# Chunks 8 and 9 of a retention kernel by the DMA crossbar, with GpSimd holding the later loads

## The chip, the cores and the metric

One core of a Trainium2 chip. The metric is the device time of one launch in microseconds (us). Every comparison is with runs of the kernel before on the same chip, in the same rounds except for e6 to e8 (see The experiments); a ratio is the mean time of one kernel's fast runs over that of the other's fast runs of the same rounds, so it is not quite the ratio of the medians that are quoted beside it. The runs list one core, so there is no second one to compare its clock with, and "fast" here means not over 1.5% above the fastest run of the same kernel.

Words: SBUF is the core's memory for tiles, PSUM the memory, in banks, to which the products of this kernel go. "By the DMA crossbar" is said of a transfer that transposes (`dma_start_transpose` in the code). "To land" is to arrive, told from the issue of the transfer. TensorE "stands" while it waits between two products.

## The reference

A recurrent retention layer, then a gated feed-forward layer on its output. Shapes: q, k, v are 4 x 8 x 768 x 64 (batch, heads, tokens, head dimension), the feed-forward goes 512 to 1536 to 512 over 3,072 tokens.

```python
for t in range(S):                                     # retention, per head
    state = gamma * state + outer(k[t], v[t])
    y[t]  = scale * q[t] @ state
x    = y.transpose(0, 2, 1, 3).reshape(B * S, H * D)   # 3072 x 512
out  = (sigmoid(x @ w_gate) * (x @ w_val)) @ w_out
```

## The kernel before

The retention is done in 24 chunks of 128 tokens, six for each of the four sequences. The feed-forward takes four chunks (512 tokens, a "tile" t, six in all) at a time; while it works on tile t, blocks of two chunks each prepare the next tiles between its groups of products. The code takes both k and q into its products with the head dimension on the partitions, so each chunk's k and q are transposed: on TensorE, with a copy out of PSUM by ScalarE (chunks 4 to 9; chunks 0 to 3 have a path of their own), or by the DMA crossbar (chunks 10 to 23). In the profile of before one transpose on TensorE took 220 ns and a chunk's eight in a row 0.45 us, 56 ns each; the copy took 1.03 us of ScalarE per chunk.

```python
    def load_kq(g):                                    # GpSimd issues all loads, in order
        kn[g] = ld.tile([C, H, D], BF16, tag="kn", name="kn")        # 10 buffers
        qn[g] = ld.tile([C, H, D], BF16, tag="qn", name="qn")
        nc.gpsimd.dma_start(out=kn[g], in_=src(k, g))
        nc.gpsimd.dma_start(out=qn[g], in_=src(q, g))

    def transposes(g):                                 # by TensorE: 8 transposes, one copy
        tp = bank([128, 2 * NP, C], BF16)
        for i, x in enumerate((kn[g], qn[g])):
            for p in range(NP):
                nc.tensor.transpose(tp[:, i * NP + p, :], pair(x, p), ident)
        qkT[g] = at.tile([128, 2 * NP, C], BF16, tag="qkT", name="qkT", bufs=6)
        nc.scalar.activation(qkT[g], tp, AX.Copy)

    def xbar(g):                                       # by the crossbar, from the SyncE queue
        qkT[g] = ld.tile([128, 2 * NP, C], BF16, tag="qkX", name="qkX", bufs=8)
        for i, x in enumerate((kn[g], qn[g])):
            nc.sync.dma_start_transpose(out=qkT[g][:, i * NP:(i + 1) * NP, :],
                                        in_=x.rearrange("s h d -> s (h d)"))

    def casts(g):                                      # ScalarE: running state to bf16
        for i in range(g, g + 2):
            if i % NCH < NCH - 1:
                state_out(i, za[i])

    def block(done, new):                              # new: scores, state; done: y of the pair before
        for g in olds: inter(g)                        # y  = q @ cast state
        for g in news: scores(g)                       # needs qkT[g]
        for g in olds: intra(g)                        # y += masked scores @ v
        ...
        for i, g in enumerate(news):
            if g % NCH < NCH - 1:                      # the last chunk of a sequence has no state product
                state(g, zz[new][:, i], True)

    plan = {                                           # tile: (after which group, step)
        0: [..., (15, step_t, 8)],                     # step_t: transposes and v's scaling
        1: [(0, casts, 6), (1, step_t, 9), (3, block, 6, 8), (5, casts, 8), ...
```

In tile 1 the first six column groups are done in halves of 256 tokens, since only half of its input is there.

Of the kernel before, what the change touches and what calls it, by code (L numbers as in the profile page):

```python
# [9 lines left out]
F32 = mybir.dt.float32  # L10
BF16 = mybir.dt.bfloat16
# [6 lines left out]
def kernel(  # L18
# [10 lines left out]
    nc = tc.nc  # L29
    B, H, S, D = q.shape  # L30
    N_TOK, D_MODEL = out.shape
    D_FF = moe_w_gate.shape[1]
    C = 128
    NCH = S // C
    NP = H // 2
# [5 lines left out]
    ctx.enter_context(tc.manual_schedule())  # L41
    const = ctx.enter_context(tc.tile_pool(name="const", bufs=1))
    wpool = ctx.enter_context(tc.tile_pool(name="wpool", bufs=1))
    ld = ctx.enter_context(tc.tile_pool(name="ld", bufs=10))
    at = ctx.enter_context(tc.tile_pool(name="at", bufs=2))
    ffn = ctx.enter_context(tc.tile_pool(name="ffn", bufs=3))
    pz = ctx.enter_context(tc.tile_pool(name="pz", bufs=1, space=bass.MemoryType.PSUM))
# [2 lines left out]

    NG = B * NCH
    NT = N_TOK // 512
    XBAR = 10
    qn, kn, vf = {}, {}, {}

    def src(x, g):
        b, c = divmod(g, NCH)
        return x[b, :, c * C:(c + 1) * C, :].rearrange("h s d -> s h d")

    def load_v(g):  # L60
        vf[g] = ld.tile([C, H, D], F32, tag="vf", name="vf", bufs=8)
        nc.gpsimd.dma_start(out=vf[g], in_=src(v, g))  # L62

    def load_kq(g):
        kn[g] = ld.tile([C, H, D], BF16, tag="kn", name="kn")
# [4 lines that stand above are left out]
    def load_chunk(g):  # L70
        load_kq(g)
        load_v(g)
# [77 lines left out]
    xT, vs, qkT, sc, stA, stB, y, zbds = {}, {}, {}, {}, {}, {}, {}, {}  # L150
    zz, za = {}, {}

    def bank(shape, dt=F32):
        return pf.tile(shape, dt, tag="ff", name="ff")
# [12 lines left out]
    def xbar(g):  # L167
# [4 lines that stand above are left out]
# [68 lines left out]
    def x_cols(t, kk, lo, hi):  # L240
        if hi - lo == 512:
            return xT[t][:, :, kk, :]
        half = lo // 256
        return xT[t][:, half, kk, lo - half * 256:hi - half * 256]
# [29 lines left out]
    def new_run_T():  # L274
        return at.tile([128, NP, 2, C], BF16, tag="qkT", name="qkT", bufs=6)
# [104 lines left out]
    def up(t, n1, lo=0, hi=512, between=None):  # L380
        if t not in hT:
            hT[t] = ffn.tile([128, NFF, 512], BF16, tag="hT", name="hT", bufs=2)
        ps = []
        for w in (wg, wv):
            u = bank([128, 512])
            for kk in range(KT):
                nc.tensor.matmul(u[:, lo:hi], w[:, kk, n1 * 128:(n1 + 1) * 128], x_cols(t, kk, lo, hi),  # L387
                                 start=(kk == 0), stop=(kk == KT - 1))
            ps.append(u)
        if between:  # L390
            between()
        gs = ffn.tile([128, 512], F32, tag="gs", name="gs")
        nc.scalar.activation(gs[:, lo:hi], ps[0][:, lo:hi], AX.Sigmoid)  # L393
        nc.vector.tensor_tensor(hT[t][:, n1, lo:hi], gs[:, lo:hi], ps[1][:, lo:hi], op=ALU.mult)  # L394

    def up_columns(t, n1s, lo, hi, rows=1):
        if t not in hT:
            hT[t] = ffn.tile([128, NFF, 512], BF16, tag="hT", name="hT", bufs=2)
        n = hi - lo
        us = [bank([128, 512]), bank([128, 512])]  # L400
        for row in range(rows):
            for w, u in zip((wg, wv), us):
                for i, n1 in enumerate(n1s):
                    for kk in range(row * KT // rows, (row + 1) * KT // rows):
                        nc.tensor.matmul(u[:, i * n:(i + 1) * n], w[:, kk, n1 * 128:(n1 + 1) * 128],  # L405
                                         x_cols(t, kk, lo, hi), start=(kk == 0 and (rows == 1 or i == 0)),
                                         stop=(kk == KT - 1), skip_group_check=rows > 1)
        ps = [u[:, :len(n1s) * n] for u in us]
        gs = ffn.tile([128, 512], F32, tag="gs", name="gs")
        g = gs[:, :len(n1s) * n]  # L410
        nc.scalar.activation(g, ps[0], AX.Sigmoid)
        nc.vector.tensor_tensor(hT[t][:, n1s[0]:n1s[-1] + 1, lo:hi], g.rearrange("p (i n) -> p i n", n=n),
                                ps[1].rearrange("p (i n) -> p i n", n=n), op=ALU.mult)
# [18 lines left out]
    def keep_on(n, u):  # L432
        for _ in range(n):
            nc.tensor.matmul(u, ident, ident4, start=True, stop=True)  # L434

    def last_down(t):
        row = t * 512 + 384
        first = 0
        for i, width in enumerate((256, 128, 128)):
            o = bank([128, 512])  # L440
            for n1 in range(NFF):
                nc.tensor.matmul(o[:, :width], hT[t][:, n1, 384:512], wo[:, n1, first:first + width],  # L442
                                 start=(n1 == 0), stop=(n1 == NFF - 1))
            ob = ffn.tile([128, width], F32, tag=f"ob{width}", name="ob", bufs=2)
            if i == 1:
                nc.scalar.copy(ob, o[:, :width])
                nc.scalar.dma_start(out=out[row:row + 128, first:first + width], in_=ob)
            else:
                nc.vector.tensor_copy(ob, o[:, :width])
                nc.sync.dma_start(out=out[row:row + 128, first:first + width], in_=ob)  # L450
            first += width
# [14 lines left out]
    load_gate_val(2)  # L466
    scale_run(1, nc.gpsimd)
    warm = bank([128, 4, 128])
    keep_on(8, warm)
    kT[0], qT[0], kT[1], qT[1] = (new_run_T() for _ in range(4))  # L470
    transpose_run(kr[0], kT[0], [nc.scalar])
    state_run(0)
# [58 lines left out]
    def ups(t):  # L531
        return [lambda n1=n1: up(t, n1) for n1 in range(NFF)]

    def downs(t):
        return [lambda sm=sm, i=i: down(t, sm, i) for sm in range(4) for i in range(2)]

    plan = {
        0: [(9, step_t, 4), (10, step_t, 5), (11, block, None, 4), (12, step_t, 6), (13, casts, 4), (13, step_t, 7),
            (14, block, 4, 6), (15, step_t, 8)],
        1: [(0, casts, 6), (1, step_t, 9), (3, block, 6, 8), (5, casts, 8), (7, scale_v, 10), (9, scale_v, 11),  # L540
            (11, block, 8, 10), (13, casts, 10), (14, scale_v, 12), (15, scale_v, 13), (18, block, 10, 12),
            (20, casts, 12)],
        2: [(0, scale_v, 14), (1, scale_v, 15), (4, block, 12, 14), (6, casts, 14), (11, scale_v, 16),
            (12, scale_v, 17), (16, block, 14, 16), (18, casts, 16)],
        3: [(3, scale_v, 18), (4, scale_v, 19), (6, block, 16, 18), (8, casts, 18), (12, scale_v, 20),
            (13, scale_v, 21), (15, block, 18, 20), (17, casts, 20)],
        4: [(3, scale_v, 22), (4, scale_v, 23), (6, block, 20, 22), (8, casts, 22), (14, block, 22, None)],
        5: [],
    }
    for t in range(NT):  # L550
        groups = ups(t) + downs(t)
        if t == NT - 1:
            groups[-2:] = [lambda: last_down(t)]
        if t == 0:
            groups = groups[4:]
            for g in range(8, 12):
                load_chunk(g)
        if t == 1:
            groups[:6] = [lambda n1=n1: up(1, n1, 0, 256) for n1 in range(6)]
            groups[6:6] = [lambda n1=n1: up_columns(1, range(n1, n1 + 2), 256, 512) for n1 in range(0, 6, 2)]  # L560
            for g in range(12, 16):
                load_chunk(g)
        if t == 2:
            load_chunk(18)
            load_chunk(19)
        if t == 3:
            load_chunk(22)
            load_chunk(23)
        for i, group in enumerate(groups):
            if t == 1 and i == 0:  # L570
                for g in range(XBAR, 12):
                    xbar(g)
            if i == len(groups) - 9:
                for g in range(4 * t + 8, 4 * t + 12):
                    if 12 <= g < NG:
                        xbar(g)
            if t == 1 and i == len(groups) - 4:
                load_chunk(16)
                load_chunk(17)
            if t == 2 and i == len(groups) - 4:  # L580
                load_chunk(20)
                load_chunk(21)
            group()
            for at_group, step, *g in plan[t]:
                if at_group == i:
                    step(*g)
# [30 lines left out]
```

## Time and profile before

| | before |
|---|---|
| median of 4 runs | 231.56 us (231.24 to 231.97) |
| span of the profiled run | 229.2 us |
| TensorE busy | 220.8 us, 96% |
| first product of tile 1's first half group | 53.22 us |
| first half group after the block of chunks 6 to 9 | 59.94 us |

The lines of the page and of the chain are in the prediction below. A row of the chain reads: start, length, what the run waited for or did at that time. L387 and L405 are the up-projections, L423 the down-projection, L163 the transposes on TensorE, L184 the scores, L196 the product with the state (inter), L233 the product with v (intra), L202 the new state. In the changed kernel each of these lines has one number less.

One more view of the kernel before gives, for a stretch of time, the busy time of each engine and, as the last three numbers, TensorE's granted clock, the DMA share and the GB/s that the DMA engines moved. From 35 to 50 us, where the loads of chunks 6 to 11 run:

```profile
35.00:50.00 15.00, 15.00 (x123) 8.20 (x123) 6.87 (x12) 7.49 (x11) 13.48 (x16) 1.00 1.90 230
```

### The profile page before, as it was taken

The page shows a single profiled execution, that of the slowest core. Times are in us where ns is not written, and L with a number is a line of the kernel's source. Part 1 is how long each engine was busy: PE and PEld are TensorE (multiplying, and loading weights), DVE is VectorE, ACT ScalarE, POOL GpSimd, SP SyncE. Part 2 cuts the span into 40 slices and gives each one's busy share as a digit, 9 for nine tenths or more (in the row PEclk, how much of TensorE's full clock was granted, in tenths as well). Part 3 has the DMA queues.
Part 4 walks back from the last instruction along what each step waited for, and adds up shares of the span by engine and source line. Part 5 has one row for each costly group of instructions (what it writes and reads, how often), then busy time and mean ns, then how long its engine had stood idle before and what let it go on. Part 6 is the DMA issues. An engine that isn't in the chain of part 4 may idle for free.

```text
span 229.2 us, 4493 instructions
## 1 busy us (share of the span) xinstructions
PE 220.8 (96%) x1814; PEld 118.5 (52%) x1814; DVE 117.7 (51%) x223; ACT 89.0 (39%) x163; POOL 77.2 (34%) x99
## 2 busy tenths in 40 slices
PE   4889999999999999999999999999999999999994
PEld 1458544567775454454445445445445454444444
DVE  5587334358975927558426267637267520243301
ACT  5785332556362423426321532623432512434221
POOL 7899956998634462733410000000000000000000
PEclk9999999999999999999999999999999999999999
DMA  7999999999999999999999353012100012100022
GB/s 135 212 197 196 198 206 207 239 240 243 188 130 108 166 169 149 271 147 118 118 170 205 94 112 26 0 50 88 51 0 3 0 46 94 46 0 0 3 92 92
DMA packets 75476, 27.55 MB, mean 120 GB/s; under 512 B 62016, under 2 KB 71104, under 8 KB 75456
## 3 DMA queue, kind: packets, MB, share of 16 engines
q0 software_dynamic: 55440, 16.78, 68.6%
q1 hardware_dynamic: 19872, 10.43, 25.8%
q8 instruction: 14, 0.23, 0.4%
q10 hardware_dynamic: 144, 0.07, 0.1%
q14 instruction: 6, 0.05, 0.1%
HBM read 28.31 MB, written 6.29 MB: 151 GB/s over the span
## 4 chain that ended last, share of the span: by engine, by line
PE 89%; DMA 5%; ACT 2%; POOL 1%; DVE 1%; issue 1%; DVEq 0%; ACTq 0%
PE ff L387 50%; PE ff L423 26%; PE ff L405 4%; DMA wv<-in_moe_w_val_dram 3%; PE ff L233 2%; PE ff L184 2%; DMA vr<-in_v_dram 2%; PE ff L196 1%; PE ff L442 1%; PE ff L163 1%; PE z L202 1%; ACT zbd L208 1%; ACT qkT L165 1%; DVE vsr L279 1%; ACT gs L393 0%
## 5 line engine op out<-in xcount | busy, mean ns | idle before, releaser
L394 DVE TENSOR_TENSOR hT<-gs,ff 128x512 bf16<-128x512 f32 (+1 forms) x70 | 45.4, 656 | 61.2 <-PE ff L387 58.7
L387 PE MATMUL ff<-xT,wg 128*128 128x512 bf16 (+1 forms) x280 | 68.5, 367 | 0.0
L387 PE MATMUL ff<-xT,wv 128*128 128x512 bf16 (+1 forms) x280 | 68.5, 367 | 0.0
L393 ACT ACTIVATE gs<-ff 128x512 f32<-128x512 f32 (+1 forms) x70 | 40.0, 573 | 70.2 <-PE ff L387 64.2
L423 PE MATMUL ff<-wo,hT 128*128 128x512 bf16 x276 | 62.2, 380 | 0.0
L387 PEld LDWEIGHTS <-wv 128*128 128x128 bf16 x280 | 27.3, 98 | 29.9 <-DMA wv<-in_moe_w_val_dram 0.3
L423 PEld LDWEIGHTS <-hT 128*128 128x128 bf16 x276 | 26.4, 98 | 30.5
L387 PEld LDWEIGHTS <-wg 128*128 128x128 bf16 x280 | 26.8, 98 | 28.5
L428 ACT COPY ob<-ff 128x512 f32<-128x512 f32 x23 | 13.5, 585 | 49.0 <-PE ff L423 48.9
L62 POOL DMA_DIRECT2D vf<-in_v_dram x20 | 18.1, 903 | 24.6 <-DMA qn<-in_q_dram 7.9
L251 DVE TENSOR_TENSOR xT<-ff,taby 128x512 bf16<-128x512 f32 x20 | 12.9, 686 | 23.7 <-PE ff L233 23.7
L67 POOL DMA_DIRECT2D kn<-in_k_dram x20 | 17.9, 894 | 9.1 <-PE ff L387 4.6
L68 POOL DMA_DIRECT2D qn<-in_q_dram x20 | 17.8, 892 | 4.2 <-DMA wo<-in_moe_w_out_dram 1.6
L208 ACT CAST zbd<-za 64x256 bf16<-64x256 f32 x38 | 15.3, 403 | 7.7 <-DVE za L220 4.8
L175 DVE TENSOR_TENSOR vs<-vf,tabv 128x512 bf16<-128x512 f32 x20 | 13.4, 686 | 3.0 <-DMA vf<-in_v_dram 3.0
L189 DVE TENSOR_TENSOR stA<-ff,causal 128x512 bf16<-128x512 f32 x20 | 13.6, 682 | 0.0
L190 DVE TENSOR_TENSOR stB<-ff,causal 128x512 bf16<-128x512 f32 x20 | 13.6, 682 | 0.0
L434 PE MATMUL ff<-ident 128*128 128x512 bf16 x14 | 5.2, 504 | 3.0 <-POOL ident masks.py:199 3.0
L165 ACT ACTIVATE qkT<-ff 128x1024 bf16<-128x1024 bf16 x6 | 6.1, 1025 | 2.8 <-PE ff L163 2.7
L405 PE MATMUL ff<-xT,wg 128*128 128x256 bf16 x48 | 6.2, 273 | 0.7 <-DMA wg<-in_moe_w_gate_dram 0.7
L405 PE MATMUL ff<-xT,wv 128*128 128x256 bf16 x48 | 6.2, 273 | 0.2 <-DMA wv<-in_moe_w_val_dram 0.2
L233 PE MATMUL ff<-stB,vs 128*64 128x128 bf16 x80 | 6.3, 222 | 0.0
(85 smaller groups left out, 144.8 us busy)
## 6 DMA issues: line engine op xcount, KB each, us to landing
out_dram<-ob SPq DMA_DIRECT2D x23, 256.0 KB, 2.1
vf<-in_v_dram POOLq DMA_DIRECT2D x20, 256.0 KB, 10.7
kn<-in_k_dram POOLq DMA_DIRECT2D x20, 128.0 KB, 11.9
qn<-in_q_dram POOLq DMA_DIRECT2D x20, 128.0 KB, 11.6
wg<-in_moe_w_gate_dram POOLq DMA_DIRECT2D x6, 256.0 KB, 7.1
wv<-in_moe_w_val_dram POOLq DMA_DIRECT2D x6, 256.0 KB, 7.8
wo<-in_moe_w_out_dram POOLq DMA_DIRECT2D x4, 384.0 KB, 9.5
vr<-in_v_dram SPq DMA_DIRECT2D x1, 512.0 KB, 4.3
```

What stands on the lines that cost most here:

```text
L62: nc.gpsimd.dma_start(out=vf[g], in_=src(v, g))
L67: nc.gpsimd.dma_start(out=kn[g], in_=src(k, g))
L68: nc.gpsimd.dma_start(out=qn[g], in_=src(q, g))
L189: nc.vector.tensor_tensor(stA[g], sc[g][0], causal4, op=ALU.mult)
L190: nc.vector.tensor_tensor(stB[g], sc[g][1], causal4, op=ALU.mult)
L208: nc.scalar.copy(zbd[g % 4][half, :, half], z[half])
L387: nc.tensor.matmul(u[:, lo:hi], w[:, kk, n1 * 128:(n1 + 1) * 128], x_cols(t, kk, lo, hi), start=(kk == 0), stop=(kk == KT - 1))
L393: nc.scalar.activation(gs[:, lo:hi], ps[0][:, lo:hi], AX.Sigmoid)
L394: nc.vector.tensor_tensor(hT[t][:, n1, lo:hi], gs[:, lo:hi], ps[1][:, lo:hi], op=ALU.mult)
L405: nc.tensor.matmul(u[:, i * n:(i + 1) * n], w[:, kk, n1 * 128:(n1 + 1) * 128], x_cols(t, kk, lo, hi), start=(kk == 0 and (rows == 1 or i = ...
L423: nc.tensor.matmul(o, hT[t][:, n1, sm * 128:(sm + 1) * 128], wo[:, n1, :], start=(n1 == 0), stop=(n1 == NFF - 1))
L428: nc.scalar.copy(ob, o)
```

## The change

The intent: take the transposes of chunks 8 and 9 off TensorE as well, and keep the loads of later chunks from crowding the transposes. For the latter, GpSimd copies one element out of a transposed chunk before it issues the loads two chunks on; the copy is written to start once that transpose has landed, and in the profile of the changed kernel the seven copies stood 59.0 us in all for landings (`POOL gate L553 <- DMA qkX<-qn`). Fewer buffers do for k, q and v then.

```diff
-    ld = ctx.enter_context(tc.tile_pool(name="ld", bufs=10))
+    ld = ctx.enter_context(tc.tile_pool(name="ld", bufs=4))
-        vf[g] = ld.tile([C, H, D], F32, tag="vf", name="vf", bufs=8)
+        vf[g] = ld.tile([C, H, D], F32, tag="vf", name="vf", bufs=6)
-    keep_on(8, warm)
+    keep_on(9, warm)
 ...
-            (14, block, 4, 6), (15, step_t, 8)],
-        1: [(0, casts, 6), (1, step_t, 9), (3, block, 6, 8), (5, casts, 8), (7, scale_v, 10), ...
+            (14, block, 4, 6), (15, scale_v, 8)],
+        1: [(0, casts, 6), (2, scale_v, 9), (4, block, 6, 8), (6, casts, 8), (10, scale_v, 10), ...
 ...
+    gate = const.tile([1, 1], BF16, name="gate")
+
+    def load_behind(g):
+        nc.gpsimd.tensor_copy(gate, qkT[g - 2][0:1, 2 * NP - 1, 0:1])
+        load_chunk(g)
+        load_chunk(g + 1)
+
+    ahead = {(0, 14): [(xbar, 8), (xbar, 9), (load_behind, 10)],
+             (1, 0): [(xbar, 10), (xbar, 11), (load_behind, 12), (xbar, 12), (xbar, 13), (load_behind, 14)],
+             ...
-            groups[:6] = [lambda n1=n1: up(1, n1, 0, 256) for n1 in range(6)]
+            groups[:8] = [lambda n1=n1: up(1, n1, 0, 256) for n1 in range(8)]
```

More of the change, by code (lines that the diff above doesn't have):

```diff
@@ L52 @@
     NT = N_TOK // 512
-    XBAR = 10
     qn, kn, vf = {}, {}, {}
@@ L538 @@
         0: [(9, step_t, 4), (10, step_t, 5), (11, block, None, 4), (12, step_t, 6), (13, casts, 4), (13, step_t, 7),
-            (14, block, 4, 6), (15, step_t, 8)],
-        1: [(0, casts, 6), (1, step_t, 9), (3, block, 6, 8), (5, casts, 8), (7, scale_v, 10), (9, scale_v, 11),
-            (11, block, 8, 10), (13, casts, 10), (14, scale_v, 12), (15, scale_v, 13), (18, block, 10, 12),
-            (20, casts, 12)],
-        2: [(0, scale_v, 14), (1, scale_v, 15), (4, block, 12, 14), (6, casts, 14), (11, scale_v, 16),
+            (14, block, 4, 6), (15, scale_v, 8)],
+        1: [(0, casts, 6), (2, scale_v, 9), (4, block, 6, 8), (6, casts, 8), (10, scale_v, 10), (11, scale_v, 11),
+            (12, block, 8, 10), (14, casts, 10), (16, scale_v, 12), (17, scale_v, 13), (20, block, 10, 12),
+            (22, casts, 12)],
+        2: [(3, scale_v, 14), (4, scale_v, 15), (6, block, 12, 14), (8, casts, 14), (11, scale_v, 16),
             (12, scale_v, 17), (16, block, 14, 16), (18, casts, 16)],
@@ L549 @@
     }
+    gate = const.tile([1, 1], BF16, name="gate")
[5 more added lines that the diff above has]
+             (1, 0): [(xbar, 10), (xbar, 11), (load_behind, 12), (xbar, 12), (xbar, 13), (load_behind, 14)],
+             (2, 0): [(xbar, 14), (xbar, 15), (load_behind, 16)],
+             (2, 11): [(xbar, 16), (xbar, 17), (load_behind, 18)],
+             (3, 0): [(xbar, 18), (xbar, 19), (load_behind, 20)],
+             (3, 11): [(xbar, 20), (xbar, 21), (load_behind, 22)],
+             (4, 0): [(xbar, 22), (xbar, 23)]}
     for t in range(NT):
@@ L555 @@
             groups = groups[4:]
-            for g in range(8, 12):
-                load_chunk(g)
+            load_chunk(8)
+            load_chunk(9)
         if t == 1:
-            groups[:6] = [lambda n1=n1: up(1, n1, 0, 256) for n1 in range(6)]
-            groups[6:6] = [lambda n1=n1: up_columns(1, range(n1, n1 + 2), 256, 512) for n1 in range(0, 6, 2)]
-            for g in range(12, 16):
-                load_chunk(g)
-        if t == 2:
-            load_chunk(18)
-            load_chunk(19)
-        if t == 3:
-            load_chunk(22)
-            load_chunk(23)
-        for i, group in enumerate(groups):
-            if t == 1 and i == 0:
-                for g in range(XBAR, 12):
-                    xbar(g)
-            if i == len(groups) - 9:
-                for g in range(4 * t + 8, 4 * t + 12):
-                    if 12 <= g < NG:
-                        xbar(g)
-            if t == 1 and i == len(groups) - 4:
-                load_chunk(16)
-                load_chunk(17)
-            if t == 2 and i == len(groups) - 4:
-                load_chunk(20)
-                load_chunk(21)
+            groups[:8] = [lambda n1=n1: up(1, n1, 0, 256) for n1 in range(8)]
+            groups[8:8] = [lambda n1=n1: up_columns(1, range(n1, n1 + 2), 256, 512) for n1 in range(0, 8, 2)]
+        for i, group in enumerate(groups):
+            for step, g in ahead.get((t, i), ()):
+                step(g)
             group()
```

## The prediction

Passages of the record that rested on no trace or run of this case are cut from the text below, and from the expectation of e7, and each cut is marked. No term of the forecast's sum is among them: it stays -0.90 - 1.18 + 0.03 = -2.05 us. The 1.03 us per copy that its part 2 uses is the trace's, given above under The kernel before. Why transposes land later beside loads is not shown by any trace here; that they do is, with a median of 9.5 us over the whole run of before against 2.4 us from 120 to 140 us, where no load is issued.

> **What bounds the kernel now.** I read the busy shares first, then the chain that ended last, then the waits of TensorE, then the chain in order of time around the place that the change touches, and last the DMA landings of the transposes. The page of the kernel before (busy time per engine with its share of the span; then the chain's shares):
>
> ```profile
> PE 220.8 (96%) x1814; PEld 118.5 (52%) x1814; DVE 117.7 (51%) x223; ACT 89.0 (39%) x163; POOL 77.2 (34%) x99
> PE 89%; DMA 5%; ACT 2%; POOL 1%; DVE 1%; issue 1%; DVEq 0%; ACTq 0%
> ```
>
> TensorE is busy 220.8 of 229.2 us and carries 89% of the chain. The rest of the chain is mostly the start: loads of v and of a weight up to 15.9 us. After that there is little idle time to win; only work taken off TensorE, or the few places where it stands, can shorten the run. One such place is the chain in order of time (start us, us, what) between 52.9 and 60 us, where the transposes of chunks 8 and 9 lie:
>
> ```profile
> 52.94 0.45 PE ff L163 x8
> 53.38 1.75 PE ff L387 x16
> 55.13 0.45 PE ff L163 x8
> ...
> 56.07 0.40 ACT zbd L208
> 56.48 0.41 ACT zbd L208
> 56.89 0.01 issue
> 56.91 0.38 ACT gs L393
> 57.29 0.50 ACT qkT L165
> 57.79 0.30 issue
> 58.09 0.68 ACT gs L393 x2
> 58.77 0.04 issue
> 58.81 0.38 PE ff L184 x7
> 59.19 0.57 PE ff L233 x16
> ```
>
> The reader is to see two things. Each chunk transposed on TensorE costs 0.45 us of its time (eight matmuls). And from 56 to 58.8 us the chain runs over ScalarE, not TensorE: the casts, a sigmoid and the copy of chunk 9's transposes out of PSUM (L165) hold up the scores of chunks 8 and 9. The timeline of TensorE has the up-projection end at about 57.17 and the first product of the scores' successor (L233) at 59.12. Between lie 4 inter products (0.22 us by the chain's 0.22 for four) and 16 score products (0.55 us for 16). So 59.12 - 57.17 - 0.77 = 1.18 us is standing time.
>
> [...] The transposes' time from issue to landing (min/median/max us), first in the whole run, then from 120 to 140 us where no load is issued:
>
> ```profile
> DMA to landing us min/median/max: 2.4/9.5/13.1
> ```
> ```profile
> DMA to landing us min/median/max: 2.4/2.4/4.1
> ```
>
> Alone, 128 KB land in 2.4 us, against 2.1 us for a plain 256 KB store[...]; beside loads they take about four times as long[...]. That is what the gate is for: it keeps the next loads out of the way of the transposes.
>
> **The change part by part.**
> 1. Chunks 8 and 9 leave TensorE: 16 transposes, 2 x 0.45 = 0.90 us off the path, because TensorE is the path there.
> 2. Their two copies leave ScalarE (about 1.03 us each). The 1.18 us of standing before the scores had ScalarE as its cause; without 2.06 us of copies in 53.4 to 58.2 us, and with the block one group (0.88 us) later, I take it as gone: -1.18 us. The same wait for chunk 7's copy at 49.2 stays.
> 3. The second tile's first eight column groups, instead of six, are done in halves. Two groups of 512 columns cost 2 x 1.73 = 3.46 us (0.865 us for four matmuls, by the starts in the timeline); in halves 4 x 0.435 + 2 x 0.875 = 3.49 us: +0.03 us.
> 4. One more warming matmul at the start, about 0.4 us. TensorE then waits 0.44 us for the first k load anyway, and the chain there runs over v and a weight load until 15.9 us: 0.
> 5. Four more crossbar transposes, 1.3 us of the SyncE queue each, and seven tiny GpSimd copies as gates. SyncE and GpSimd are not on the path: 0 by themselves.
> 6. k and q get 4 buffers in place of 10, v 6 in place of 8. The order of instructions shows that the loads of chunk 8 now wait for TensorE to finish the state of chunk 4 (44.6 us by the chain: 44.37 + 0.25); before, k of chunk 8 was issued at 41.8 us. So the loads of 8 and 9 move back some 2.8 us.
> 7. The later blocks move one to two groups back. TensorE executes the same products in another order: 0 as long as nothing is late.
>
> Sum without a new wait: -0.90 - 1.18 + 0.03 = -2.05 us, so 229.6 us.
>
> **The rivals.**
> *A: the transposes of 8 and 9 come late and stall TensorE.* Loads are issued 0.88 us apart on GpSimd, so q of chunk 9, fifth of six, is issued at 44.6 + 4 x 0.88 = 48.1 us. Loads issued in 39 to 50 us landed after 6.2 to 7.7 us with a full queue behind them; with the pause of 2.8 us I estimate 5.5 to 6.5. It lands at 53.6 to 54.6. Its transpose is issued then and, the gate holding chunk 10 back until chunk 8 is through, should land 2.4 to 4 us later: 56 to 58.6 us. TensorE starts the second tile 0.45 us earlier than before (52.8), needs five half groups of 0.875 us, then 0.22 for inter and 0.27 for chunk 8's scores: it wants chunk 9 at 57.7. So the stall is 0 to 1 us, my mean 0.6. If the transposes are as slow as beside the old loads (7.4 to 12 us), it would be 3.5 to 5 us and eat the whole gain: 231 to 234 us.
> *B: the chain of gates is slower than TensorE later.* One turn of two chunks is six issues (5.3 us), about 5.5 us to landing and 2.5 us for the last transpose, with overlap about 11 to 13 us. The blocks want a pair at about 57, 71, 85, 102, 119, 136, 152 and 171 us (old chain shifted, with the new group numbers), never less than 13.5 us apart. So it keeps up; only the pair 10/11, wanted at 71 and ready by my estimate at 68 to 71, is close. Such a stall would not add to the first, since the gates do not wait for TensorE; the later of the two decides. Each would make 230 to 232 us.
> *C: the gain is hidden elsewhere.* For: 1.18 us of standing is short, and VectorE is fairly full from 50 to 65 us (3.7 to 4.7 of each 5 us by the table of stretches), so its masks might take ScalarE's place in holding TensorE. Against: the block now has three further half groups behind it before the whole-width work needs its y, where it had two. If only part 1 pays: 230.8 us.
> *D: gain over 2%.* It would need 4.6 us; TensorE's busy time forbids it.
>
> **Range and chances.** From 231.68: -2.05, +0.6 for A and some +0.1 for B and C, gives 230.3 us. Low end, all gains and no stall with noise of the runs (231.24 to 231.97 before): 229.2. High end, a stall of about 3 us at the first or second pair: 232.6. Slower by 2% (236.3) would need a stall of 6.5 us or a collapse of the transposes' pace: 0.03. Faster by 2% (227.1): 0.02. Within 2%: 0.95.
>
> **What the profile after would show.** L163's successor has 32 matmuls instead of 48 and the copy out of PSUM 4 instead of 6 of that shape. In the waits of TensorE, a wait of the score products for the DMA of qkX, of 0 to 1 us, near 57 us; over 2 us means rival A. The ScalarE pieces between 56 and 58.8 us are gone from the chain. GpSimd shows seven gate copies, waiting for qkX; the landings of the transposes have a median well under 9.5 us (4 or less if the gate works); the DMA row stays busy until about 165 us instead of 137. The prediction is wrong if the scores of chunks 8 to 11 wait long for the crossbar, or if TensorE stands just as long there for ScalarE or VectorE.

## The result, and the profile after

The changed kernel takes 230.89 us (median of 4 runs, 230.62 to 231.42) against 231.56 us: ratio 0.9973, interval 0.9949 to 0.9998. The time lies in the predicted range, but the predicted gain was 1.4 us and the measured one is 0.6 us. In a second set of five rounds (e1 below) it was smaller still.

The page of the changed kernel, busy times and shares of the chain:

```profile
PE 219.9 (96%) x1815; PEld 119.1 (52%) x1815; DVE 117.9 (51%) x224; ACT 87.0 (38%) x162; POOL 78.9 (34%) x106
PE 84%; DMA 10%; POOL 2%; issue 1%; DVE 1%; SPq 1%; DVEq 0%
```

TensorE works 0.9 us less, as the prediction had it. But TensorE's share of the chain fell from 89% to 84% and that of the DMA rose from 5% to 10%: transfers now hold TensorE. The chain in order of time shows where:

```profile
46.02 8.70 DMA kn<-in_k_dram
54.72 0.02 issue
54.73 1.19 SPq L169
55.92 0.04 issue
55.97 3.58 DMA qkX<-qn
59.54 0.14 issue
59.68 0.40 PE ff L183 x8
```

The load of chunk 9's k takes 8.7 us from its issue; then come the issues of its transposes on SyncE, then 3.58 us for the last one to land, and only then chunk 9's scores. The waits of TensorE (engine, line, for whom: us in total, times, longest) include three that the kernel before does not have:

```profile
PE ff L183 <- DMA qkX<-qn: 0.6, 1, 0.6
...
PE ff L162 <- DMA qn<-in_q_dram: 0.3, 1, 0.3
...
PE ff L386 <- DVE hT L393: 0.2, 1, 0.2
```

The second is for the load of chunk 7's q, a chunk that the change does not touch. The third is for PSUM banks: a half group of the up-projection can't start until VectorE has taken an earlier one out of its banks. The transposes themselves land as hoped; over the whole run, min/median/max us:

```profile
DMA to landing us min/median/max: 2.4/3.6/6.6
```

So the median is 3.6 us in place of 9.5. And here is the same stretch of 15 us as above:

```profile
35.00:50.00 15.00, 14.69 (x112) 7.74 (x111) 7.03 (x12) 7.24 (x11) 10.54 (x12) 1.00 1.81 207
```

207 GB/s in place of 230, in a stretch where the DMA engines are about as busy (1.81 and 1.90), and GpSimd comes to its first gate only at 48.7 us. This is the line that led to the cause.

### The profile page after: what moved, and what is told of

Read it like the earlier page. It is cut to its first block, busy times and chain, and to the rows that moved or that the text cites. A ratio compares the mean times of both kernels' runs of the same rounds, so it can differ in the third digit from the quotient of the medians.

```text
span 229.3 us, 4531 instructions
## 1 busy us (share of the span) xinstructions
PE 219.9 (96%) x1815; PEld 119.1 (52%) x1815; DVE 117.9 (51%) x224; ACT 87.0 (38%) x162; POOL 78.9 (34%) x106
## 4 chain that ended last, share of the span: by engine, by line
PE 84%; DMA 10%; POOL 2%; issue 1%; DVE 1%; SPq 1%; DVEq 0%
PE ff L386 47%; PE ff L422 23%; PE ff L404 5%; DMA kn<-in_k_dram 4%; DMA wv<-in_moe_w_val_dram 3%; PE ff L232 2%; PE ff L183 2%; DMA vr<-in_v_dram 2%; DMA qkX<-qn 2%; PE ff L195 1%; PE ff L441 1%; PE z L201 1%; DVE vsr L278 1%; SPq L169 1%; PE ff L162 0%
## 5 line engine op out<-in xcount | busy, mean ns | idle before, releaser
L393 DVE TENSOR_TENSOR hT<-gs,ff 128x512 bf16<-128x512 f32 (+1 forms) x70 | 44.8, 648 | 59.1 <-PE ff L386 53.4
L386 PE MATMUL ff<-xT,wg 128*128 128x512 bf16 (+1 forms) x280 | 67.6, 364 | 0.2 <-DVE hT L393 0.2
L386 PE MATMUL ff<-xT,wv 128*128 128x512 bf16 (+1 forms) x280 | 67.6, 364 | 0.1
L392 ACT ACTIVATE gs<-ff 128x512 f32<-128x512 f32 (+1 forms) x70 | 39.5, 567 | 67.7 <-PE ff L386 61.7
L427 ACT COPY ob<-ff 128x512 f32<-128x512 f32 x23 | 13.5, 585 | 49.2 <-PE ff L422 45.1
L553 POOL COPY gate<-qkX 1x1 bf16<-1x1 bf16 x7 | 1.6, 234 | 59.0 <-DMA qkX<-qn 59.0
L66 POOL DMA_DIRECT2D kn<-in_k_dram x20 | 17.9, 894 | 5.8 <-DMA qkX<-kn 1.5
L404 PE MATMUL ff<-xT,wg 128*128 128x256 bf16 x56 | 7.3, 273 | 1.1 <-DMA wg<-in_moe_w_gate_dram 1.1
L404 PE MATMUL ff<-xT,wv 128*128 128x256 bf16 x56 | 7.3, 273 | 0.1
L411 DVE TENSOR_TENSOR hT<-gs,ff 128x512 bf16<-128x512 f32 x7 | 4.7, 687 | 4.0 <-PE ff L404 3.9
```

The source lines that it names most:

```text
L386: nc.tensor.matmul(u[:, lo:hi], w[:, kk, n1 * 128:(n1 + 1) * 128], x_cols(t, kk, lo, hi), start=(kk == 0), stop=(kk == KT - 1))
L392: nc.scalar.activation(gs[:, lo:hi], ps[0][:, lo:hi], AX.Sigmoid)
L393: nc.vector.tensor_tensor(hT[t][:, n1, lo:hi], gs[:, lo:hi], ps[1][:, lo:hi], op=ALU.mult)
L404: nc.tensor.matmul(u[:, i * n:(i + 1) * n], w[:, kk, n1 * 128:(n1 + 1) * 128], x_cols(t, kk, lo, hi), start=(kk == 0 and (rows == 1 or i = ...
```

## The experiments

Sixteen runs were made, on three chips (e1 to e8 on one, e9 to e12 on another, e13 to e16 on a third). The runs of before are quoted with each; e5 to e8 are compared with the eleven of e1 to e4, made twelve minutes earlier on the same chip, and one more, so a drift is not excluded. The medians of before in the calls differ by up to 0.2 us (231.21 to 231.37; 231.56 in the first set), so times are compared within a call and ratios across calls. All results were correct.

### e1: the changed kernel again

> The changed kernel again, for a tighter interval and a second profile. Theory S (the standing of TensorE before the scores of chunks 8 and 9 was not removed but came back as a wait for PSUM banks of 0.6 us and a wait for the crossbar of 0.6 to 0.7 us): 0.5 to 0.8 us below the kernel before, ratio 0.9965 to 0.998. If instead the profiled run's start (0.25 us later) and its wait for q of chunk 7 (0.5 us) are part of the change and not noise, both show again; if they are noise, the wait for q of chunk 7 is absent or appears in the run of before too.

231.06 us against 231.29, ratio 0.9991 (0.9976 to 1.0006): a gain of 0.2 us that is not clear of the noise. With the first set, the change as it stands is worth something like 0.2 to 0.6 us. In this profile tile 0's down-projection began 0.3 us later than in the first, the delay by chunk 7's q was 0.25 us by the starts in the timeline (its transposes took 0.70 in place of 0.45 us; the table of waits doesn't list it), and the scores waited 1.20 us for the crossbar.

### e2: six buffers for k and q

```diff
-    ld = ctx.enter_context(tc.tile_pool(name="ld", bufs=4))
+    ld = ctx.enter_context(tc.tile_pool(name="ld", bufs=6))
```

> The changed kernel with 6 buffers for k and q in place of 4, so that the loads of chunks 8 and 9 do not wait for TensorE. Theory T1 (late crossbar is what ate the gain): the wait of the scores for the crossbar near 59 us goes, and the time falls by 0.5 to 0.8 us against the changed kernel (about 230.2). Rival T2 (the PSUM banks and ScalarE take the place of that wait): the wait for the crossbar goes, but TensorE then stands for VectorE or ScalarE, and the time falls by less than 0.3 us.

231.45 us against 231.29, ratio 1.0008 (0.9992 to 1.0025). The wait of the scores is still there, and longer:

```profile
PE ff L183 <- DMA qkX<-qn: 1.2, 1, 1.2
```

So the buffers are not what makes chunks 8 and 9 late. The timeline of GpSimd explains why: in the changed kernel the load of chunk 8's k was issued at 42.86 us and the fifth load (chunk 9's q) at 46.89, not at 44.6 and 48.1 as the prediction had them. The line there shows what ended GpSimd's short wait (last column):

```profile
42.86 0.87 POOL L66 DMA_DIRECT2D kn<-in_k_dram  x1 [0.20 <-PE ff L162]
```

It waited for transposes (L162), not for a state product: the first buffer to come free is that of chunk 5, the last of its sequence, which has no state product. With six buffers the issue was at 42.59 us. The loads start early enough; they land late.

### e3 and e4: the state casts two groups later, alone and with six buffers

```diff
-        1: [(0, casts, 6), (2, scale_v, 9), (4, block, 6, 8), ...
+        1: [(2, casts, 6), (2, scale_v, 9), (4, block, 6, 8), ...
```

> The changed kernel with the state casts of chunks 6 and 7 two groups later in ScalarE's order (after the third half group, not the first), so that ScalarE does not stand for VectorE at their head. T2: the waits of 0.6 us for PSUM banks at 57 us go. But if the crossbar comes at 59.5 us anyway (T1), the block waits just as long for it, and the time is within 0.3 us of the changed kernel.

> Both edits together. If the two waits hide each other (each alone gives little), this gives 1.0 to 1.4 us against the changed kernel, so about 229.6, which is the sum of the prediction. If T1 alone is right it is no better than the 6 buffers alone; if T2 alone is right, no better than the later casts alone.

e3: 230.75 us against 231.29, ratio 0.9995 (0.9962 to 1.0029); one of its runs, the profiled one, was at a clock of 0.993 and took 233.4 us, which widens the interval (in its trace the clock was at half from 61.4 to 64.8 us, right behind the waits for the crossbar). e4: 230.87 us, ratio 0.9997 (0.9968 to 1.0027), with one such run too. In both profiles the wait for PSUM banks near 57 us is gone and a wait for the crossbar remains (2.2 us over two places in e3, 0.63 us in e4). Neither reaches the 229.6 us hoped for; inconclusive as times, and as profiles they say that the crossbar's lateness is left.

### e5: the kernel before again, one look

> The kernel before once more, for a second profile of it. In five profiles of the changed kernel and its variants q of chunk 7 lands 1.7 us later than in the one profile of before (48.5 against 46.7 us), and already the weights land 0.3 to 0.8 us later. If this is noise of the runs, it shows here too or lies between; if it comes with the change, q of chunk 7 lands at about 46.7 us again and TensorE does not wait for it.

A single run of 230.65 us, whose state is unknown. Its profile served as the control: chunk 7's q landed at 46.5 us, as in the first profile of before (46.7), and TensorE did not wait for it. In each of the five profiles of the changed kernel and its variants so far it landed at 48.5 to 48.7 us. The slower loads therefore came with the change and not with the run.

### e6: only the casts of the kernel before moved

```diff
-        1: [(0, casts, 6), (1, step_t, 9), (3, block, 6, 8), ...
+        1: [(2, casts, 6), (1, step_t, 9), (3, block, 6, 8), ...
```

> The kernel before with only the state casts of chunks 6 and 7 moved two groups later in ScalarE's order. If the 1.18 us of standing before the scores was ScalarE being held at these casts by VectorE, part or most of it goes: 0.4 to 1.0 us faster. If it was the copies of the transposes, as the prediction had it, nothing changes (within 0.3 us).

231.17 us against 231.29, ratio 0.9996 (0.998 to 1.0012): nothing. The product with the state then waits for the casts itself:

```profile
PE ff L196 <- ACT zbd L208: 0.5, 1, 0.5
```

The two copies of transposes are still in ScalarE's queue, and moving the casts alone only moves the wait.

### e7: chunks 8 and 9 by the crossbar, without the rest

```diff
-    XBAR = 10
+    XBAR = 8
-            (14, block, 4, 6), (15, step_t, 8)],
-        1: [(0, casts, 6), (1, step_t, 9), ...
+            (14, block, 4, 6), (15, scale_v, 8)],
+        1: [(0, casts, 6), (1, scale_v, 9), ...
+            if t == 0 and i == 14:
+                xbar(8)
+                xbar(9)
```

> The kernel before with chunks 8 and 9 by the crossbar and nothing else of the change: old buffers, no gate, old places of the blocks. Theory: the transposes [...]land after 9 to 12 us instead of 4 to 6, and the scores wait for them at 57 us until 62 to 65 us: 4 to 7 us slower than before, and the gates are what makes the crossbar usable here. Rival: the gates do little at this place, the wait is 2 us or less and the time is within 1 us of before.

239.50 us against 231.29, ratio 1.0352 (1.0335 to 1.0369): 8 us slower. The waits of TensorE, and the clock row of the page:

```profile
PE ff L184 <- DMA qkX<-qn: 7.5, 2, 4.2
```
```profile
PEclk9999999999559999999999999999999999999999
```

The four transposes landed after 9.2 to 11.6 us (from 49 us on), beside loads of chunks 10 to 12 that nothing held; in the changed kernel those of chunks 8 and 9 landed after 3.6 to 6.4 us. TensorE stood 7.5 us, and two slices of the page ran at half the granted clock (0.68 on average from 55 to 70 us); the loss, 8.2 us by the medians, exceeds the wait. Loads issued beside them took longer still: those of chunks 11 and 12 landed after 13.5 to 17.9 us. So holding the loads, in one way or another, is what makes the crossbar usable at this place (e16 bears this out: there the buffers alone hold them). The granted clock fell at 60.3 us, 3.1 us into the first of two waits (3.3 and 4.2 us); in e3 and e10 it fell right behind waits of 2.2 us in all. What makes it fall, no run here shows.

### e8: later casts, and the block one half group later

```diff
-        1: [(0, casts, 6), (2, scale_v, 9), (4, block, 6, 8), (6, casts, 8), ...
+        1: [(2, casts, 6), (2, scale_v, 9), (5, block, 6, 8), (7, casts, 8), ...
```

> The changed kernel with the later casts, and the block of chunks 6 to 9 one half group later. If the wait for the crossbar (0.6 to 1.6 us in four profiles) is what is left of the lost gain, 0.87 us of it fills with a half group: 0.4 to 0.8 us faster than the later casts alone (230.7), about 230.1. If y of chunks 6 and 7 then comes too late for the whole-width columns, or loads simply set the pace, it is within 0.2 us of that.

230.42 us against 231.29, ratio 0.9966 (0.9946 to 0.9985). The scores no longer wait for the crossbar. This treats the symptom: the loads are as slow as in the changed kernel (all profiles at this placement of the tiles, e8's among them, moved 203 to 207 GB/s from 35 to 50 us; see the next part).

### e9, e10, e11: where the tiles lie

Why should loads of chunk 7, or of the weights, be slower in the changed kernel? Its one new tile is the gate: 2 bytes, which take 32 in SBUF, allocated ahead of the weights. In the built programs the first weight starts at byte 53,120 of each partition before and at 53,152 after, and every tile behind it is moved by the same 32 bytes.

```diff
 e9 (e11: 64 in place of 32)
-    gate = const.tile([1, 1], BF16, name="gate")
+    gate = const.tile([1, 32], BF16, name="gate")
-        nc.gpsimd.tensor_copy(gate, qkT[g - 2][0:1, 2 * NP - 1, 0:1])
+        nc.gpsimd.tensor_copy(gate[:, 0:1], qkT[g - 2][0:1, 2 * NP - 1, 0:1])
 e10, in the kernel before
+    pad = const.tile([1, 1], BF16, name="pad")
+    nc.vector.memset(pad, 0.0)
```

> The changed kernel with the gate's tile 64 bytes long in place of 2 (which takes 32). In the changed kernel the weights, k, q and v start 32 bytes further on in SBUF than before (53,152 in place of 53,120 for the first weight), no longer at a multiple of 64; with this edit they are at multiples of 64 again. Theory P (placement: the 32 bytes slow the loads): q of chunk 7 lands at 46.5 to 47.5 us, not 48.5, TensorE does not wait for it, the crossbar's last transpose for chunk 9 lands 1 us or more earlier, and the time falls by 0.6 to 1.2 us. Rival N (the slower loads come from elsewhere): landings as in the changed kernel, and the time within 0.3 us.

> The kernel before with an unused tile of 2 bytes (32 in SBUF) ahead of the weights, and nothing else. Theory P: the weights' last load lands 0.5 us later than before (about 28.4 us against 27.8), q of chunk 7 at about 48.4 us, TensorE waits for it 0.2 to 0.6 us, and the time rises by 0.3 to 1.0 us. Rival N: landings and time as before, within 0.3 us.

> The changed kernel with the gate's tile 128 bytes long, so that all loaded tiles start at multiples of 256 bytes. If what counts is that the start is a multiple of 64, as for e9 (within 0.2 us of it); if the transfers gain further from 256, landings another 0.3 us or more earlier.

The three came with the same runs of before, 231.37 us.

| kernel | loaded tiles start, past a multiple of 256 bytes | GB/s, 35 to 50 us | chunk 7's q lands, us | median us | ratio to before |
|---|---|---|---|---|---|
| before | 128 | 230 | 46.7 | 231.37 | 1 |
| e10 before, 32 bytes more | 160 | 204 | 48.5 | 232.65 | 1.0046 (1.0009 to 1.0083) |
| changed (e1) | 160 | 205 | 48.6 | 231.06 | 0.9991 |
| e9 changed, 64 byte gate | 192 | 205 | 48.4 | 231.34 | 0.9988 (0.9957 to 1.0018) |
| e11 changed, 128 byte gate | 0 | 230 | 47.4 | 230.22 | 0.9949 (0.9919 to 0.998) |

The rows for the stretch from 35 to 50 us, of the kernel before with 32 bytes of padding:

```profile
35.00:50.00 15.00, 14.75 (x111) 7.78 (x112) 7.01 (x12) 7.11 (x11) 11.54 (x14) 1.00 1.81 204
```

of the changed kernel with the 64 byte gate:

```profile
35.00:50.00 15.00, 14.63 (x111) 7.75 (x112) 6.99 (x12) 7.29 (x11) 10.54 (x12) 1.00 1.82 205
```

and with the 128 byte gate:

```profile
35.00:50.00 15.00, 14.89 (x118) 8.11 (x118) 7.05 (x12) 7.30 (x11) 10.74 (x13) 1.00 1.93 230
```

The last number of each row is the one to compare. Thirty-two bytes of padding slow the kernel before by about a tenth in this stretch of loads and cost it about 1 us (one of its runs, the profiled one, was slow and is not in the ratio; its granted clock was at half from 76.6 to 80.0 us, after the stretch that is read here). In that profile TensorE lost 0.32 us to chunk 7's q (by the starts) and stood 2.2 us for the late transposes of chunk 11, a wait that before does not have; the clock fell right behind it:

```profile
75.85 0.40 PE L184 MATMUL ff<-qkX 64*128 64x128 bf16 x8 [2.23 <-DMA qkX<-qn]
```

VectorE's and ScalarE's instructions took the same time on the moved tiles (gate times value, L394: 687 ns with and without the padding; the sigmoids of 128x512, L393: 597 ns in before and, moved by the same 32 bytes, in the changed kernel), so the tiles' own use is not what became slower.

My expectation that a multiple of 64 would do is refuted: e9 is as slow as the changed kernel. A multiple of 128 does. With it, chunk 9's last transpose landed at 57.0 us in place of 59.5, TensorE waited neither for it nor for chunk 7's q, and the gain of the change against before went from 0.2 to 0.6 us up to 1.15 us; against e9, e11 is 0.7 us faster by the means of the runs. In the stretch from 20 to 35 us, mostly weights, 200 or 201 GB/s moved in all of these, so the placement did not show there.

The kept traces hold every DMA packet with its size, queue and time (no view lists them), and they tell which loads it slows. From 35 to 50 us, the packets of 4,096 bytes, which are v's, took 172 to 181 ns on average in the nine profiles with tiles at 0 or 128, and 259 to 273 ns in the nine at 160 or 192. Those of 128 bytes, which are k's and q's, took 32 ns in all eighteen, and those of 512 bytes, the weights', 60 to 61 ns over the whole run. GpSimd's first load of v goes into a tile that the 32 bytes did not move, and its packets took 185 to 192 ns everywhere. So v's transfers are what the placement slows; k and q, whose loads are issued between v's, land later without being slower themselves.

A start 128 past a multiple of 256 did as well as a multiple of 256 here: the nine profiles at 0 or 128 moved 227 to 232 GB/s from 35 to 50 us, the nine at 160 or 192 moved 203 to 207. Why a target that starts at 160 or 192 takes v's packets longer, no run here shows.

### e12: the 64 byte gate with e8's two moves

```diff
 e9's edit and e8's edit together
```

> The changed kernel with the 64 byte gate, the later casts and the block one half group later together. If the loads then come early enough anyway, no better than the 64 byte gate with the block in its place plus what the casts' wait was (0 to 0.3 us); if each of the three waits found (for q of chunk 7, for PSUM banks, for the crossbar) was worth its time, about 229.5 to 230.0 us, 1.3 to 1.8 below before, which is near the sum of the prediction.

230.01 us against 231.37, ratio 0.9937 (0.9908 to 0.9966). The moves of e8 are worth 1.3 us over e9 here: where the loads are slow, later casts and a half group more for the crossbar pay together; no run at this placement has them apart.

### e13: the kernel before with 128 bytes of padding

```diff
+    pad = const.tile([1, 64], BF16, name="pad")
+    nc.vector.memset(pad, 0.0)
```

> The kernel before with an unused tile of 128 bytes ahead of the weights: all later tiles move from 128 past a multiple of 256 to a multiple of 256. If a multiple of 128 is all that counts: landings as before (q of chunk 7 at 46.5 to 47.5 us), time within 0.3 us of before, and the gain of e11 belongs to the change. If 256 counts, 0.5 us or more faster than before.

231.00 us against 231.21, ratio 0.9992 (0.9979 to 1.0005); 230 GB/s in the stretch. The kernel before lay well already, so the gain of e11 is not one that padding would give the kernel before.

### e14 and e15: the right placement with later casts, and with the later block too

```diff
 e14: e11's edit and e3's; e15: e11's edit and e8's
```

> The changed kernel with the 128 byte gate and the casts of chunks 6 and 7 two groups later. If the early casts hold ScalarE's sigmoids and with them the PSUM banks, the waits of 0.2 and 0.35 us for VectorE near 57 and 59 us go: 0.3 to 0.6 us faster than e11 (230.2), about 229.8. If the inter product of chunk 7 then waits for the casts, as in e6, it is within 0.2 us.

> The 128 byte gate with the later casts and the block one half group later: all the waits found are met at once. 229.4 to 229.8 us, the predicted sum of 2.05 us less what the waits of 0.16 us at other places cost. If it is no better than e14, the place of the block only served to hide the late crossbar.

e14: 229.72 us against 231.21, ratio 0.9935 (0.9922 to 0.9948). e15: 229.28 us, ratio 0.9911 (0.9898 to 0.9924). Both beat both kernels. The intervals of e11 and e14 overlap, so that the casts matter is read from the profiles; e15 is 0.4 us faster than e14. e15 is 1.9 us faster than before, which is nearly the predicted sum of 2.05. In e15 the chain in order of time runs over TensorE alone where it had run over ScalarE before and over the DMA in the changed kernel:

```profile
53.66 5.24 PE ff L386 x48
58.90 0.22 PE ff L195 x4
59.12 0.55 PE ff L183 x16
59.68 0.57 PE ff L232 x16
60.24 0.25 PE z L201 x16
```

In e11, with the casts in their early place, a half group still waited (idle time and its cause in the last column):

```profile
56.82 0.60 PE L386 MATMUL ff<-xT,wg 128*128 128x256 bf16 x4 [0.20 <-DVE hT L393]
```

ScalarE's lines of e11 show why. The four casts stood 1.36 us for VectorE's sums and then took 1.65 us, and the four sigmoids, for which the emptying of the banks waits, came only behind them:

```profile
55.41 1.65 ACT L207 CAST zbd<-za 64x256 bf16<-64x256 f32 x4 [1.36 <-DVE za L217]
57.08 1.32 ACT L392 ACTIVATE gs<-ff 128x256 f32<-128x256 f32 x4
```

The standing time can be put into one table, from the timelines of TensorE: from the first half group of tile 1 to the first half group after the block, less the work between (0.4365 us for each half of a gate or value product, by e15's starts; 0.45 us for a chunk's transposes; 1.69 us for the block, from e15, where it ran without a gap).

| kernel | first half group, us | after the block, us | work between, us | standing, us |
|---|---|---|---|---|
| before | 53.22 | 59.94 | 3.49 + 0.45 + 1.69 | 1.09 |
| changed | 53.29 | 60.83 | 4.37 + 1.69 | 1.48 |
| changed (e1) | 53.36 | 61.41 | 4.37 + 1.69 | 1.99 |
| e11, loads in time | 52.97 | 60.06 | 4.37 + 1.69 | 1.03 |
| e14, casts later too | 52.97 | 59.35 | 4.37 + 1.69 | 0.32 |
| e15, block later too | 53.49 | 60.42 | 5.24 + 1.69 | 0 by construction |

The 1.09 us before the scores were not removed by taking the copies off ScalarE; with the loads in time (e11) 1.03 us are still there, now as waits for PSUM banks behind the early casts. They go when the casts move as well (e14), and the last 0.32 us (a wait for a sigmoid) with the later block (e15). That this part is gone by itself in e15 follows from the choice of e15 as the measure of the work; what stands on its own is that its chain has no other engine from 53.66 to 60.49 us.

### e16: the gate's copy taken out, placement kept

```diff
 with e11's tile
-        nc.gpsimd.tensor_copy(gate, qkT[g - 2][0:1, 2 * NP - 1, 0:1])
+        nc.gpsimd.memset(gate[:, 0:1], 0.0)
```

> The changed kernel with the 128 byte tile, but the gate's copy reads nothing (a write of a constant in its place), so that only the 4 and 6 buffers hold the loads. If the gate is what keeps the loads off the transposes: the transposes of chunks 8 and 9 land after 7 to 12 us in place of 4 to 6, the scores wait 3 us or more, 3 to 8 us slower than e11. If the small buffers do the same service, within 0.5 us of e11.

230.59 us against 231.21, ratio 0.9971 (0.9959 to 0.9983). Not the 3 to 8 us that I expected. Chunk 10's loads were held anyway, until 52.15 us, by a state product on TensorE that still read the buffer; the profile has no wait for the crossbar. With 4 buffers in place of 10, the buffers do most of what the gate was for. By the same reckoning as in the table above, TensorE stood 1.03 us between the same places (53.21 and 60.30 us), as in e11. Against e11 (0.9949, on another chip) the gate is worth 0 to 0.5 us; the intervals overlap, so this stays open.

## Why the prediction was right or wrong

- **TensorE's 0.90 us for 16 transposes: right.** A chunk's transposes took 0.45 us from start to start (52.77 to 53.22 us in before), and two chunks' are gone. Busy time fell by 220.8 - 219.9 = 0.9 us too, but with the halves and one more warming matmul (0.4 us) it should have fallen by only 0.5, so this match is partly luck.
- **The 1.18 us of standing at the scores: the step that failed in part 2.** "I take it as gone" was wrong. The copies of chunks 8 and 9 were one cause among two in a queue; without them, the casts of chunks 6 and 7 held the sigmoids and thus the PSUM banks for as long: TensorE stood 1.03 us in e11, and 1.48 and 1.99 us in the two profiles of the changed kernel, where the crossbar came late as well. Rival C named this kind of wait, with VectorE in ScalarE's place, but gave it almost no weight (+0.1 us with B). Only both together, with the loads in time, bring the gain (e14, e15); e6 shows that later casts alone bring none to the kernel before.
- **Part 6 and rival A: right in kind, wrong in two terms.** The loads of chunks 8 and 9 did not wait for the state of chunk 4: the first was issued at 42.9 us, not 44.6. Yet they landed later than estimated, because a load took 7.9 to 8.7 us, not "5.5 to 6.5". The fifth (chunk 9's q) was issued 1.2 us earlier than predicted and landed at 55.3 us, 0.7 to 1.7 us later. The stall that followed was 0.6 and 1.2 us in two profiles, against an estimate of 0 to 1, mean 0.6.
- **The term that was missing.** No step of the prediction asked where the new tile would lie. Its 32 bytes moved the targets of all later loads off a multiple of 128, took a tenth off the loads' rate from 35 to 50 us, added a wait for chunk 7's q (0.48 us of delay in the profile: its transposes took from 47.84 to 48.77 us, 0.93 in place of 0.45 us) and made the crossbar late. All nine profiles at such a placement have this delay, of 0.2 to 0.55 us, and none of the other nine has it. e10 shows it in the kernel before, e11 undoes it in the changed one.
- **Rival B: right that it would not bind.** After 62 us no wait for the crossbar shows in the profile of the changed kernel.
- **The transposes' landings: right.** Median 3.6 us ("4 or less if the gate works"). But in e16, where the gate held nothing, it was 4.0 us, so the small buffers would have done much the same, and the number is no proof of the gate.

The sum with measured terms, for the profiles: -0.90 (transposes) + 0.03 (halves) + 1.48 - 1.09 (standing) + 0.48 (chunk 7's q) = 0.0 us, and the spans of the two profiled runs are 229.2 and 229.3 us. For e15: -0.90 + 0.03 - 1.09 = -1.96 us, with one more half group that only changes places; measured 231.21 - 229.28 = 1.93 us. That it fits to 0.03 us is luck: e15's profiled run was the slowest of its five (229.70 us, span 228.0, 1.2 below the profile of before), and its tile 1 began at 53.49 us, 0.5 us later than in e14. The medians of the changed kernel are 0.2 and 0.7 us below before's, though the profiles show no gain: the profiled run of before (230.92 us) was faster than all four timed ones (from 231.24).

What stays open: how much the gate's copy is worth beside the small buffers; and why v's packets lose by a misplaced start while k's, q's and the weights' do not.

## What to carry to other kernels

Before blaming a schedule for slower loads, compare where the tiles start: one tiny tile ahead of the big ones can move every DMA target, so give small tiles sizes that keep the rest at multiples of 128 bytes (0 and 128 past a multiple of 256 gave 227 to 232 GB/s here, 160 and 192 gave 203 to 207). Allocating them last was not tried. When two things queue ahead of a wait, removing one shows little; look in the timeline at what else would still stand there, and remove both before judging. A transpose by the crossbar took no TensorE time here and landed in 2.4 us where nothing else was loading, but after 9.2 to 11.6 us beside unheld loads (e7); hold the later loads, with a small number of buffers or with a gate, and put the consumer where the landing times of the trace say it is ready.
